# A Fourier-mixing and feed-forward kernel: one scheduling region instead of two, half of a weight conversion moved later, small copies on another engine

## The chip, the cores and the metric

The kernel runs on one core of a Trainium2 chip. The metric is device time in microseconds (us): 2882.8 us is the median of seven runs, which lie between 2877.8 and 2884.53.

A core has a matrix engine (PE in the profile; its weight loads are PEld), a vector engine (DVE), an activation engine (ACT), a general engine (POOL, GpSimd in the code) and a sync engine (SP) that here only issues transfers. Every engine takes its own instructions strictly in order, and a waiting instruction holds up all that stand behind it on that engine. Transfers are issued by SP, ACT and POOL, and all run on the core's 16 DMA engines.

## The reference

`x` has 8 batches of 3008 rows and 256 columns. The rows are transformed, multiplied by a filter, and transformed back; the result goes through a two-layer block with the activation h - tanh(h).

```python
X = np.fft.rfft(x, axis=1)
Y = X * (filt_r + 1j * filt_i)[None]
x2 = np.fft.irfft(Y, n=3008, axis=1).reshape(24064, 256)
h = x2 @ w_in                       # 256 -> 2048
out = (h - np.tanh(h)) @ w_out      # 2048 -> 256
```

`w_in`, `w_out`, and the result of the product with them, start as float64; the kernel gets the weights as 64-bit integers.

## The kernel before, in words

**The transform.** 3008 is 64 x 47. A first pass (`first0` for batch 0, `first` for the others) multiplies 64-row blocks of `x` by a constant matrix and stores the result in DRAM (`ct1`). A middle pass loads it back (`a2`), multiplies with constants (`fg`, loaded in eight slots of four matrices), applies the filter, multiplies again and stores to `ct2`. A last pass (`last`) loads `ct2` (`e2`) and multiplies once more; its result `ut` feeds the two-layer block. Batches are worked in five groups: 0, then 1 and 2, 3 and 4, 5 and 6, then 7.

**The weights.** Each weight matrix is converted from float64 bits to float32 on the chip (`converted`, L191 to L223) in jobs of 128 x 512 numbers. A job is a 512 KB load (`raw`, L197, issued by SP), DVE masks and shifts (L204, L207, L210), two ACT operations (L205, L209), a DVE step that adds the low word (L211, the last reader of `raw`), and DVE steps that assemble the result (L214, L215, L222). Two jobs make a quarter (256 of `w_in`'s or `w_out`'s 1024 paired columns or rows), and `sums` (L253) then builds four sums on POOL. Quarters 0 to 3 are `w_in`, 4 to 7 are `w_out`. `weights` (L225) is a generator: each `next` does a piece of a job, and it starts the load of a job two ahead.

**Two parts, each a region of its own** (`with tc.manual_schedule()` at L861 and at L973). Inside a region instructions stand in program order.

The *first part* does batch 0's first pass (`first0`), then a loop over j = 0 to 15 that is batch 0's middle pass. For every second j it loads the next slot of `a2` and `fg` on SP, and issues the six filter transfers two slots ahead on POOL (`filters_of`, L803, into one of three buffers). Per j there are two DVE products with the filter (`uv` L922, `zs` L923), matmuls (L896, L898, L915), an ACT copy (`e1`, L901) and its store (L902). At odd j ACT duplicates the filter rows (`double_filters`, L838) and builds a turned and negated copy of the constants (`turned`, L845, tile `gx`). One `next(ws)` per j advances the conversion of quarters 0 to 4. Near the end `first(1)` begins for the second group: two `x_sb` loads at j = 14, and after the loop EARLY = 3 of its 24 steps.

The *dense part* is a software pipeline over U, four per chunk of output columns. In step U, `up(U)` does the first product, `shrink(U-1)` the activation, `down(U-2)` the second product. Each U has five slots `t(0)` to `t(4)`. A slot can carry one step of the next group's first or middle pass (their due positions are evenly spread, `steps`), one step of the conversion of quarters 5 to 7 (`late`, at slots 0, 2 and 4), and one step of `copies` (slots 1 and 3 from U = 1 on). `copies` (`filters_d`, L951) writes zeros and then all of the filter into a DRAM tensor `filt_d`, laid out for the later middle passes: eight steps of six to ten transfers (L814), issued by SP. `down` of quarter 5 runs at U = 3, of 6 at U = 4, of 7 at U = 5; quarter 4 is used from U = 2.

In the dense part SP also issues the `x_sb` loads of `first` (two chunks ahead, three buffers), the `raw` loads (two buffers), the `e2` loads, and all output stores.

Of the kernel before, what the change touches and what calls it, by code (L numbers as in the profile page):

```python
# [41 lines left out]
EARLY = 3  # L42
# [100 lines left out]
def kernel(  # L143
# [47 lines left out]
    def converted(tiles, src, dsts, queue):  # L191
# [13 lines left out]
        ACT.activation(ft, it, AF.Identity, bias=1.0, scale=2.0 ** -20)  # L205

        V.tensor_scalar(out=pt, in0=hi, scalar1=20, scalar2=0x7FF,  # L207
                        op0=ALU.logical_shift_right, op1=ALU.bitwise_and)
        ACT.activation(pt, pt, AF.Relu, bias=exp_b)  # L209
        V.tensor_scalar(out=st, in0=hi, scalar1=-2 ** 31, scalar2=None, op0=ALU.bitwise_and)  # L210
        V.scalar_tensor_tensor(out=ft, in0=lo, scalar=2.0 ** -52, in1=ft,  # L211
                               op0=ALU.mult, op1=ALU.add)
        yield
# [11 lines left out]
    def weights(tiles, quarters, ahead):  # L225
# [36 lines left out]
        for k in range(len(jobs)):  # L262
            next(began[k])
            if k and k % 2 == 0:
                sums(quarters[k // 2 - 1])
            if k + ahead < len(jobs):
                began.append(start(k + ahead))
            yield
            next(began[k])
            yield  # L270
# [77 lines left out]
    def middle(p, z):  # L348
# [58 lines left out]
        yield  # L407

# [347 lines left out]
    with tc.tile_pool(name="tr", bufs=2) as tr:  # L756
        with tc.tile_pool(name="pro", bufs=1) as pro, \
# [45 lines left out]
            def filters_of(c, to=None):  # L803


                n = 4 if c < NK // 4 - 1 else 3

                def put(row, m, v, i, n_s, src, off, dims):
                    if to is None:
                        dst = t[IM * v + row:IM * v + row + m, v, i:i + n_s, :]  # L810
                    else:
                        dst = dram(to, ((row * 2 + v) * NK + 4 * c + i) * DM,
                                   [[2 * NK * DM, m], [DM, n_s], [1, DM]])
                    (G if to is None else nc.sync).dma_start(dst, dram(src.tensor, off, dims))  # L814

                if to is None:
                    t = filt[c % 3]


                    if c < 3:  # L820
                        for v in range(2):
                            G.memset(t[IM * v + 32:IM * v + 64, v], 0.0)
                    if n == 3:
                        G.memset(t[IM:IM + 1, 1, 3], 0.0)
                for row, m in ((0, LO), (LO, 16), (LO + 16, HI - 16)):
                    sign = 1 if row < LO else -1
                    r0 = 4 * c + 1 + NQ * row if row < LO else NQ * (row - LO + 1) - 1 - 4 * c
                    for v, src in enumerate((filt_r, filt_i)):
                        put(row, m, v, 0, n, src, r0 * DM, [[NQ * DM, m], [sign * DM, n], [1, DM]])
                if n == 3:  # L830
                    for v, src in enumerate((filt_r, filt_i)):
                        put(v, LO - v, v, 3, 1, src, v * NQ * DM,
                            [[NQ * DM, LO - v], [DM, 1], [1, DM]])
                        put(LO, HI, v, 3, 1, src, NQ // 2 * DM,
                            [[NQ * DM, HI], [DM, 1], [1, DM]])
                return None if to is not None else t
# [8 lines left out]
            def turned(g3, t):  # L845


                ACT.copy(t[0:RP], g3[IM:IM + RP])
                ACT.mul(t[IM:IM + RP], g3[0:RP], -1.0)
# [11 lines left out]
            with tc.manual_schedule():  # L861
                nc.sync.dma_start(wf1, wf1_d)
                V.memset(near_b, B)
                V.memset(exp_b, -896.0)
                xs = [load_x0(0, (0, 4, 8)), load_x0(1), load_x0(2)]
                ws = weights(tiles0, range(5), 2)

                pad = pro.tile([64, DM], F32, name="pad")
                G.memset(pad, 0.0)
                G.dma_start(dram(ct1[0], NR * 64 * DM, [[DM, 64], [1, DM]]), pad)  # L870
                fts = {0: filters_of(0)}
                gx = [pro.tile([IM + RP, 4, RP2], F32, name=f"gx{k}") for k in range(2)]
                for t in gx:
                    G.memset(t[32:64], 0.0)
                mats = {0: load_slots(0, pro)}
                next(ws)
                for c in range(3):
                    for k, _ in enumerate(first0(xs[c], c)):
                        if k == 3 or k == 1 and c > 0:
                            next(ws)  # L880
                G.dma_start(s2, s2_d)
                fts[1] = filters_of(1)
                a2 = {0: load_a2(0, 0, False)}
                mats[1] = load_slots(1, pro)
                next(ws)
                double_filters(fts[0], 0)
                turned(mats[0][1], gx[0])
                waiting = []

                def back0():  # L890
                    j, uv, zs = waiting.pop(0)
                    c = j // 2
                    pe = z0("pe", [128, 2, DM])
                    for i in range(2):
                        k = (2 * j + i) % 4
                        nc.tensor.matmul(pe[0:RP2, i], mats[c][1][:, k], uv[0:IM + RP, i],  # L896
                                         start=True, stop=False)
                        nc.tensor.matmul(pe[0:RP2, i], gx[c % 2][:, k], zs[0:IM + RP, i],  # L898
                                         start=False, stop=True)
                    e1 = tr.tile([RP2, 2, DM], F32, tag="e1", bufs=2, name="e1")  # L900
                    ACT.copy(e1, pe[0:RP2])  # L901
                    ACT.dma_start(dram(ct2[0], 2 * j * RP2 * DM,  # L902
                                       [[DM, RP2], [2 * RP * DM, 2], [1, DM]]), e1)

                for j in range(NK // 2):
                    c = j // 2
                    if j % 2 == 0 and c + 1 < NK // 4:
                        a2[c + 1] = load_a2(0, c + 1, False)
                        if c + 2 < NK // 4:
                            mats[c + 2] = load_slots(c + 2, pro)  # L910
                            fts[c + 2] = filters_of(c + 2)
                    pz = z0("pz", [128, 2, DM])
                    for i in range(2):
                        k = (2 * j + i) % 4
                        nc.tensor.matmul(pz[:, i], mats[c][0][0:R2, k],  # L915
                                         a2[c][0:R2, k * DM:k * DM + DM], start=True, stop=True)
                    if waiting:
                        back0()
                    uv = tr.tile([128, 2, DM], F32, tag="uv", bufs=2, name="uv")
                    zs = tr.tile([128, 2, DM], F32, tag="zs", bufs=2, name="zs")  # L920
                    ft = fts[c][:, :, j % 2 * 2:j % 2 * 2 + 2]
                    V.tensor_mul(uv, pz, ft[:, 0])  # L922
                    V.tensor_mul(zs, pz, ft[:, 1])  # L923
                    waiting.append((j, uv, zs))
                    next(ws, None)
                    if j % 2 and c + 1 < NK // 4:
                        double_filters(fts[c + 1], c + 1)
                        turned(mats[c + 1][1], gx[(c + 1) % 2])
                    if j == NK // 2 - 2:
                        fs = first(1, z1)  # L930
                        next(fs)
                        e2s[0] = load_e2(*groups[0], None, slice(0, 48))
                back0()
                load_e2(*groups[0], e2s[0], slice(48, 64))
                for _ in range(EARLY):
                    next(fs)
                for _ in ws:
                    pass


        with tc.tile_pool(name="dn", bufs=2) as dn, \
# [9 lines left out]
            def filters_d():  # L951
# [15 lines left out]
                for c in range(NK // 4):  # L967
                    filters_of(c, filt_d)
                    yield

            late, copies = weights(tiles1, range(5, 8), 2), filters_d()
            total = 4 * len(groups)
            with tc.manual_schedule():  # L973
                for _ in last(0, z1):
                    pass
                next(late)
                for U in range(total + 2):
                    i, u = divmod(U, 4)
                    if U < total:
                        p, c = groups[i]  # L980
                        if c == 0 and u == 0:
                            units = 4 * len(CHUNKS[p])
# [9 lines left out]
                        if u == 0 and i + 1 < len(groups) and c + 1 < len(CHUNKS[p]):  # L992
                            e2s[i + 1] = load_e2(*groups[i + 1])
# [62 lines left out]
                for w in stores:  # L1056
                    store(*w)
# [37 lines left out]
```

## Time and profile before

| | us |
|---|---|
| median of seven runs | 2882.8 |
| the profiled execution, its own time | 2883.05 |
| its span in the trace | 2881.3 |
| PE busy (share of the span) | 2752.5 (96%) |
| DVE busy | 1989.4 (69%) |
| ACT busy | 1872.1 (65%) |
| POOL busy | 1743.4 (61%) |
| first matmul of `last` (L447), where the dense part begins | 116.36 |
| mean granted clock of PE | 0.982 |

The busy share is an average over stages that have different limits. PE is busy 229.2 of the first 300 us, and 2523.3 of the 2581 us from 300 on. The windows show, for each stretch of time, the busy time of each engine with its instruction count, the granted clock of PE (1.00 is full speed), the share of time that the DMA engines worked, and what they moved. In the timeline a row is start, duration, engine, line, operation, what is written and read; "q" after an engine's name marks a transfer that it issued. In the list of waits a row names the waiting engine and line, what it waited for, and us in total, times, and the longest.

### The profile page before, as it was taken

Reading aid. Unit: us, or ns where it says so; the run is one execution under the profiler, and the core shown is the slowest. Engines: PE = TensorE matmul, PEld = TensorE weight load, DVE = VectorE, ACT = ScalarE, POOL = GpSimd, SP = SyncE. Lnnn points to the kernel's source line nnn. Section 1 sums busy time; section 2 is a strip of 40 time slices with the busy share of each in tenths; the row PEclk is TensorE's granted clock in tenths of the full one; section 3 lists DMA queues with packets and bytes.
Section 4 is the critical chain, followed back from the end, with each engine's and each line's share of the span. In section 5 each row is a group of like instructions: output and inputs, shape, how many; then the busy total and the mean of one; then the engine's idle time right before and its main releaser. Section 6 shows DMA issues by size and latency. Waiting matters only on the chain.

```text
span 2881.3 us, 36469 instructions
## 1 busy us (share of the span) xinstructions
PE 2752.5 (96%) x12474; PEld 2279.7 (79%) x12474; DVE 1989.4 (69%) x2214; ACT 1872.1 (65%) x2460; POOL 1743.4 (61%) x1382
## 2 busy tenths in 40 slices
PE   5789999999999999999999999999999999999996
PEld 3467777888878787888877887888888888888885
DVE  4675666766777777766677777776777777777765
ACT  3655666666666667666666677666666666666663
POOL 4345777444677767645576777655466666555543
PEclk7889999999999999999999999999999999999998
DMA  9644443232233322232323233122233222110100
GB/s 270 180 150 118 115 107 90 66 96 75 70 81 86 74 69 54 56 86 80 87 70 73 69 83 76 36 50 62 51 76 80 55 54 55 25 27 15 29 8 16
DMA packets 328061, 217.46 MB, mean 75 GB/s; under 512 B 229085, under 2 KB 280405, under 8 KB 327674
## 3 DMA queue, kind: packets, MB, share of 16 engines
q1 hardware_dynamic: 273176, 160.50, 23.6%
q10 hardware_dynamic: 52738, 51.33, 5.9%
q0 software_dynamic: 1952, 3.22, 0.5%
q8 instruction: 100, 1.64, 0.3%
q14 instruction: 95, 0.78, 0.1%
HBM read 138.81 MB, written 79.17 MB: 76 GB/s over the span
## 4 chain that ended last, share of the span: by engine, by line
PE 69%; ACT 9%; DVE 9%; POOL 5%; issue 4%; DMA 3%; SPq 1%; ACTq 1%; DVEq 0%; POOLq 0%
PE o L590 27%; PE x L483 18%; PE z L483 8%; PE y L483 5%; PE pe L364 3%; PE pu L447 3%; DVE h L544 3%; PE pz L383 3%; ACT y L539 2%; PE pf L304 2%; ACT y L540 1%; POOL t L465 1%; ACT u L489 1%; DVE uv L398 1%; DVE h L519 1%
## 5 line engine op out<-in xcount | busy, mean ns | idle before, releaser
L590 PE MATMUL o<-t,wd 128*128 128x256 f32 (+2 forms) x3072 | 777.2, 376 | 1.8 <-POOL t L464 1.3
L544 DVE TENSOR_TENSOR h<-h,y 128x1024 f32<-128x1024 f32 (+2 forms) x384 | 589.6, 1535 | 255.9 <-ACT y L540 255.9
L462 POOL TENSOR_TENSOR t<-h 128x512 f32<-128x512 f32 (+2 forms) x192 | 240.0, 1250 | 770.5 <-DVE h L548 584.0
L590 PEld LDWEIGHTS o<-t,wd 128*128 128x128 f32 x3072 | 580.9, 191 | 74.8 <-POOL t L464 1.9
L483 PE MATMUL x<-tu,wu 128*128 128x256 f32 (+2 forms) x2304 | 591.5, 379 | 16.5 <-ACT u L489 15.5
L590 PE MATMUL o<-h,wd 128*128 128x256 f32 (+2 forms) x2304 | 583.5, 376 | 0.2 <-DVE h L548 0.2
L548 DVE SCALAR_TENSOR_TENSOR h<-sq,h 128x1024 f32<-128x1024 f32 (+2 forms) x384 | 566.6, 1476 | 20.8 <-ACT y L539 0.5
L483 PEld LDWEIGHTS x<-tu,wu 128*128 128x128 f32 x2304 | 429.5, 191 | 157.2 <-issue 72.7
L590 PEld LDWEIGHTS o<-h,wd 128*128 128x128 f32 x2304 | 432.6, 191 | 71.9 <-issue 18.5
L545 ACT ACTIVATE sq<-y,near_b 128x1024 f32<-128x1024 f32 (+2 forms) x384 | 435.4, 1134 | 5.8 <-DVE h L548 1.1
L539 ACT ACTIVATE y<-h 128x1024 f32<-128x1024 f32 (+2 forms) x384 | 400.0, 1042 | 14.8 <-ACT e L367 6.8
L489 ACT COPY s<-x 128x512 f32<-128x512 f32 (+2 forms) x192 | 110.7, 577 | 458.3 <-PE x L483 446.9
L540 ACT ACTIVATE y<-y 128x1024 f32<-128x1024 f32 (+2 forms) x384 | 399.2, 1040 | 12.2
L465 POOL TENSOR_TENSOR t<-t,h 128x512 f32<-128x512 f32 (+2 forms) x192 | 306.8, 1598 | 0.0
L489 ACT COPY u<-x 128x512 f32<-128x512 f32 (+2 forms) x384 | 219.2, 571 | 74.9 <-PE x L483 37.8
L399 POOL TENSOR_TENSOR zs<-zs,ft 128x512 f32<-128x512 f32 x112 | 166.2, 1484 | 142.1 <-ACT zs L397 142.0
L463 POOL TENSOR_TENSOR t<-h,t 128x512 f32<-128x512 f32 (+2 forms) x192 | 241.5, 1258 | 15.1
L464 POOL TENSOR_TENSOR t<-h 128x512 f32<-128x512 f32 (+2 forms) x192 | 249.5, 1300 | 0.0
L400 POOL TENSOR_TENSOR uv<-uv,zs 128x512 f32<-128x512 f32 x112 | 211.3, 1887 | 16.0 <-DVE uv L398 7.8
L483 PE MATMUL x<-ut,wu 128*128 128x256 f32 (+2 forms) x768 | 200.5, 384 | 12.2 <-DVE h L519 10.6
L483 PE MATMUL z<-tu,wu 128*128 128x256 f32 (+2 forms) x768 | 195.9, 378 | 0.5 <-DVE h L525 0.5
L499 DVE TENSOR_TENSOR h<-y,s 128x512 f32<-128x512 f32 (+2 forms) x192 | 130.3, 679 | 94.1 <-PE y L483 85.1
(113 smaller groups left out, 3303.6 us busy)
## 6 DMA issues: line engine op xcount, KB each, us to landing
a<-ct SPq DMA_DIRECT2D x64, 384.0 KB
ct<-e ACTq DMA_DIRECT2D x128, 192.0 KB
ft<-filt SPq DMA_DIRECT2D x96, 256.0 KB
out_dram<-ot SPq DMA_DIRECT2D x1408, 16.0 KB
ct<-a ACTq DMA_DIRECT2D x80, 256.0 KB
x_sb<-in_x_dram SPq DMA_DIRECT2D x69, 256.0 KB
e<-ct SPq DMA_DIRECT2D x33, 512.0 KB
fg<-fg SPq DMA_DIRECT2D x40, 392.0 KB
```

The source lines that it names most:

```text
L462: G.tensor_sub(t[0], b[0][1], b[0][0])
L463: G.tensor_sub(t[1], b[1][1], t[0])
L464: G.tensor_sub(t[2], b[1][1], b[0][1])
L465: G.tensor_sub(t[3], t[1], b[1][0])
L483: nc.tensor.matmul(bank[:, k], wu[:, q - 1, (2 * u + k) * 128:(2 * u + k + 1) * 128], rhs[q - 1], start=(first and k == 0), stop=True, ski ...
L489: ACT.copy(t, X)
L539: ACT.activation(y[k], ht[k], AF.Arctan, scale=S)
L540: ACT.activation(y[k], y[k], AF.Square)
L544: V.tensor_mul(ht[k], ht[k], y[k])
L545: ACT.activation(sq[k], y[k], AF.Square, bias=near_b, scale=A)
L548: V.scalar_tensor_tensor(out=ht[k], in0=sq[k], scalar=K, in1=ht[k], op0=ALU.add, op1=ALU.mult)
L590: nc.tensor.matmul(product(q), wd[:, q - 1, (2 * u + k) * 128: (2 * u + k + 1) * 128], rhs[q - 1][:, k], start=(u == 0 and k == 0 and q == ...
```

## The change

1. The two regions become one that spans the whole kernel.
2. `converted` now stops once more: the three DVE masks; then the two ACT operations; then all other DVE steps, L211's among them. `weights` interleaves: a step A does the masks of job k, a step B does the ACT operations of job k, the rest of job k-1, and starts the load of job k+2.
3. The first part converts quarters 0 to 3, the dense part 4 to 7. `late` runs at every slot of U = 0 and U = 1, and at slots 0, 2 and 4 after that.
4. During `first0` the conversion takes one step instead of five; four more follow after it.
5. `turned` runs on GpSimd. The zeroing of the second and third filter buffer stands ahead of `first0`, the filter transfers of slot 1 follow the first `turned`.
6. EARLY is 2. `first(1)` starts at j = 13, `e2`'s first load is at j = 15, and the last rows of `e2` are loaded after the EARLY steps, not ahead of them.
7. `copies` writes the filter in ten transfers, over all 31 rows at once, one per step, issued by GpSimd.

```diff
-EARLY = 3
+EARLY = 2
...
         V.tensor_scalar(out=st, in0=hi, scalar1=-2 ** 31, ...)
+        yield
+        ACT.activation(ft, it, AF.Identity, bias=1.0, scale=2.0 ** -20)
+        ACT.activation(pt, pt, AF.Relu, bias=exp_b)
+        yield
         V.scalar_tensor_tensor(out=ft, in0=lo, scalar=2.0 ** -52, in1=ft, ...)
-        yield
         V.tensor_scalar_min(pt, pt, 255.0)
...
-        for k in range(len(jobs)):
-            next(began[k])
-            if k and k % 2 == 0:
-                sums(quarters[k // 2 - 1])
-            if k + ahead < len(jobs):
-                began.append(start(k + ahead))
-            yield
-            next(began[k])
-            yield
+        for k in range(len(jobs) + 1):
+            if k < len(jobs):
+                next(began[k])
+            if k > 2 and k % 2:
+                sums(quarters[k // 2 - 1])
+            yield
+            if k < len(jobs):
+                next(began[k])
+            if k > 0:
+                next(began[k - 1])
+            if k + ahead < len(jobs):
+                began.append(start(k + ahead))
+            yield
...
+    def filter_rows(a, z):
+        n, src = min(z, NK - 1) - a, (filt_r.tensor, filt_i.tensor)
+        for row, m in ((0, LO), (LO, 16), (LO + 16, HI - 16)):
+            low = row < LO
+            at = a + 1 + NQ * row if low else NQ * (row - LO + 1) - 1 - a
+            for v in range(2):
+                yield v, row, m, 0, n, dram(src[v], at * DM,
+                                            [[NQ * DM, m], [DM if low else -DM, n], [1, DM]])
...
-    with tc.tile_pool(name="tr", bufs=2) as tr:
+    with tc.tile_pool(name="tr", bufs=2) as tr, tc.manual_schedule():
...
             def turned(g3, t):
-                ACT.copy(t[0:RP], g3[IM:IM + RP])
-                ACT.mul(t[IM:IM + RP], g3[0:RP], -1.0)
+                G.tensor_copy(t[0:RP], g3[IM:IM + RP])
+                G.tensor_scalar_mul(t[IM:IM + RP], g3[0:RP], -1.0)
...
-                ws = weights(tiles0, range(5), 2)
+            ws = weights(tiles0, range(4), 2)
...
-                    if j == NK // 2 - 2:
-                        fs = first(1, z1)
-                        next(fs)
-                        e2s[0] = load_e2(*groups[0], None, slice(0, 48))
-                back0()
-                load_e2(*groups[0], e2s[0], slice(48, 64))
-                for _ in range(EARLY):
-                    next(fs)
+                if j == NK // 2 - 3:
+                    fs = first(1, z1)
+                    next(fs)
+                if j == NK // 2 - 1:
+                    e2s[0] = load_e2(*groups[0], None, slice(0, 48))
+            back0()
+            for _ in range(EARLY):
+                next(fs)
+            load_e2(*groups[0], e2s[0], slice(48, 64))
...
-                for c in range(NK // 4):
-                    filters_of(c, filt_d)
+                for v, row, m, i, n, src in filter_rows(0, NK):
+                    G.dma_start(dram(filt_d, ((row * 2 + v) * NK + i) * DM,
+                                     [[2 * NK * DM, m], [DM, n], [1, DM]]), src)
                     yield
-            late, copies = weights(tiles1, range(5, 8), 2), filters_d()
+            late, copies = weights(tiles1, range(4, 8), 2), filters_d()
...
-                        if k in (0, 2, 4):
-                            next(late, None)
-                        elif U > 0:
-                            next(copies, None)
+                    if U < 2 or k in (0, 2, 4):
+                        next(late, None)
+                    if U > 0 and k in (1, 3):
+                        next(copies, None)
```

## The prediction

> **What bounds the kernel now.** I read the windows first, because the busy shares average over stages. From 300 us on PE works 2523.3 of 2581 us, and the change touches nothing that runs there. So all that it can give or take lies in the first 300 us, of which PE works 229.2. Two windows of that stretch (PE, PEld, DVE, ACT, POOL; then clock, DMA share, GB/s):
>
> ```profile
> 0.00:50.00 50.00, 21.42 (x46) 10.70 (x47) 16.66 (x36) 16.31 (x27) 21.31 (x38) 0.76 0.97 274
> 50.00:100.00 50.00, 41.24 (x150) 26.73 (x149) 40.20 (x74) 33.06 (x49) 28.52 (x47) 0.90 0.91 236
> ```
>
> The DMA engines are taken 97% and 91% of the time, every compute engine less. The first part is bound by bytes, with DVE (40.2 of 50) next. SP's timeline shows which bytes need not be there, and how the part ends:
>
> ```profile
> 16.55 3.26 SPq L197 DMA_DIRECT2D raw<-in_moe_w_out_dram  x2
> ...
> 68.25 0.39 SPq L197 DMA_DIRECT2D raw<-in_moe_w_out_dram  x1
> ...
> 77.47 0.39 SPq L197 DMA_DIRECT2D raw<-in_moe_w_out_dram  x1
> ...
> 107.20 0.32 ACTq L902 DMA_DIRECT2D ct<-e  x1
> ...
> 110.30 1.39 SPq L283 DMA_DIRECT2D x_sb<-in_x_dram  x3
> ...
> 113.64 2.05 PE L304 MATMUL pf<-x_sb,wf_sb 128*128 128x512 f32 x2 [6.16 <-DMA x_sb<-in_x_dram]
> ```
>
> The two loads at 68.25 and 77.47 are quarter 4. The two at 16.55 can only be the first loads of `late`, because quarter 4's come far later: in program order they stand behind the whole first part, but with two regions they were put 95 us ahead of it. At the end, `x_sb` for the third EARLY step waits behind `e2`'s last rows, which wait for the store of 107.20; PE stands 6.16 us, and `last` begins only at 116.36.
>
> After that the waits of PE between 110 and 330 us, and what SP waits for between 115 and 245:
>
> ```profile
> PE pf L304 <- DMA x_sb<-in_x_dram: 12.8, 4, 6.2
> PE x L483 <- ACT u L489: 12.4, 5, 3.8
> PE pe L364 <- POOL uv L400: 4.2, 1, 4.2
> ...
> SPq L197 <- DVE ft L211: 31.4, 4, 12.5
> SPq L814 <- DMA ct<-a: 25.2, 7, 6.6
> ```
>
> The largest is a load that SP issues too late; SP's queue then holds 52 filter copies (L814), which waited 25.2 us besides their issue.
>
> **The change part by part.** The sum is made against the profiled execution, 2883.05 us, which is 0.25 us from the median; I don't correct for that.
>
> *Bytes out of the first part (one region, quarter 4 later).* Four `raw` loads of 512 KB leave it: 2.1 MB. At the mean of the two windows, 255 GB/s, that is 8.2 us; at the 399 GB/s of 20 to 30 us it is 5.3. The conversion of two jobs leaves too: by the medians of its rows 0.42 + 0.42 + 0.42 + 0.69 + 0.42 + 0.69 + 0.83 = 3.9 us of DVE a job, 7.8 in all, and 2.7 of ACT. Also, ACT no longer waits for job 0 between the copies of `first0`: it stood 8.29 us before L205 at 21.84 and the last copies came at 33.5. That and the DVE time let the loop start and end earlier, but the other bytes still have to move, so I add only 1. Bounds: 0, if the pace is set by the latency of single transfers (the `e1` store of 49.96 took 11.6 us to land); 13, because DVE at 80% lets the 64 us from 43 to 107 shrink by no more than a fifth. I take **-9**, near the byte count, as the DMA row is the fullest.
>
> *End of the first part (EARLY, order of the loads).* The two remaining EARLY steps use chunks that were loaded at j = 13. After the last `e1` store (107.20, landed at 109.48) only `e2`'s last rows come: two issues of 0.4 and a landing. The nearest landings are `x_sb`, 110.30 to 113.64, 3.3 us for four times the bytes; I take 2.5. `last` then begins at 112.3 in today's times instead of 116.36: -4. The third EARLY step moves to the dense part: two matmuls of 0.43, +0.9. Together **-3.2** (bounds -4 to -1.5, if `e2` takes as long as `x_sb` and both 0.4 issues count again).
>
> *Two more jobs in the dense part.* +7.8 us of DVE and 2.7 of ACT, all at U = 0 to U = 4 (120.99 to 213.74 today). DVE is busy 65.1 of the 80 us from 120 to 200, so 15 us are free: bounds 0 and 7.8. U = 1 gets the most: three tails (L211 to L222, 2.63 each) and two sets of masks (1.26 each), 10.4 us of DVE against some 5.8 today. I take **+4**, the middle, since idle DVE time here is mostly waiting that comes in the wrong place.
>
> *The new wait for `raw`.* L211 is the last reader of a `raw` buffer, and moves from step A of job k to step B of job k+1. With two buffers, the load of job k+2 now stands in SP's queue until then, and job k+2's masks follow one step later on DVE. Between L211 and those masks DVE has L214, L215 and L222 (1.9 us) and one to three `h` operations (0.68 each): 2.6 to 4.0 us. The load needs between 3.3 (`x_sb`, half the bytes) and 5.5 (issued 125.50, its masks ran at 130.96 without a wait). So 0 to 2.9 us a job, for six jobs: 0 to +17. Behind the masks stand `h` additions that the next `up` needs; behind the waiting load stand the `x_sb` loads. Two chunks of lead and three buffers leave an `x_sb` load about three slots. I take **+3**, half a microsecond a job, as DVE runs behind PE at U = 1 anyway.
>
> *Filter copies on GpSimd.* Of the `x_sb` stalls, 4.17 us (to 200.76) and 1.94 (to 238.27) fall where SP is among the L814 copies, and after each PE's matmul groups take 1.9 instead of 1.03 until the clock is back: some 2 us more each. That is 10 in all. SP keeps the waits of the `raw` loads up to U = 3, so I take **-7**; bounds -10 and 0. On POOL ten issues at the 0.55 us of today's L814 rows make 5.5 us, within idle stretches of 10 to 14 us a U; were they slow, the four POOL sums of `shrink` (1.3 each) would wait and PE with them.
>
> The skill's page "DMA: Bandwidth & Descriptors", section "Issuing engines are not separate DMA queues", speaks against this part: all issuers share the same DMA engines, and another issuer only saves issue time, usually small. By that rule the term would be about nothing, since no bytes go away; the SP rows above (25.2 us of waiting, 52 issues of some 0.7) say that here the issue queue is the matter.
>
> *`turned` on GpSimd.* Sixteen operations of 0.51 leave ACT (33 of 50 busy, so this gives 0). On POOL each costs between 0.35 (the memset of 32 x 1024 takes 0.94; 384 columns of it) and 1.1 (the 128 x 256 sum takes 0.73, times 1.5). At most 2.2 a slot, beside six issues (3.3) and on average 1.5 of sums: 7.0 of the 8 us a slot takes now. While POOL adds, DVE's 0.42 us masks take 0.95, so DVE may lose up to 8 us, of 27 idle in the loop. Taken: 0, bounds -1 and +4.
>
> *The zeroing and slot 1's filters earlier:* POOL is idle from 10 to 31 us. 0.
>
> Sum: -9 - 3.2 + 4 + 3 - 7 = -12.2, so 2870.8; I forecast **2870** (0.45% faster). By the terms' likelier halves this case spans 2860 to 2876.
>
> The skill's page "TensorE: Matmul & The Clock Gate", Part 1, says that an idle window of some 3.4 us halves the clock; the 1.94 us stall, after which groups also took about twice as long, is shorter than that. By the page that stall would cost 2 and not 4 us.
>
> **Rivals.**
> (a) *The front is not bound by bytes*: the freed DMA time goes to latency, and the loop keeps its pace. For it: the 11.6 us landing, and DMA at 45% already at 95 us. Against: 0.97. Then -3.2 + 4 + 3 - 7 = -3: 2880, no change that can be told.
> (b) *The conversion becomes a chain* (the other side): each of six jobs waits for its load behind the job two before it, DVE stands in front of `h`, and `x_sb` is late behind the same load. For it: SP already waits 31.4 us for L211. Price: +17 from the loads; then the -7 is lost too, as SP stays blocked, and one cold start (2) is added: -9 - 3.2 + 4 + 17 + 2 = +11: 2894. It decides from a load of about 5 us on, where the wait exceeds 2 us a job.
> (c) *The front gains more*: loop down to DVE's pace (-13), hidden conversion (0), no new wait, all SP stalls gone: -13 - 3.2 - 10 = -26, so 2857.
> (d) *It doesn't do what it says*: one region changes nothing, and `late`'s loads still come early. Then half of the byte term (4.1) returns: 2875, inside the main case.
>
> **How the numbers follow.** Main case with (d) 0.60, (c) 0.13, (a) 0.15, (b) 0.12. A difference of 0.2% (5.8 us) is about what a measurement tells from none; the bounds are 2877 and 2888.6. Faster: main and (c), 0.73; same: (a), 0.15; slower: (b), 0.12. The range goes from 2853 ((c) with the outer bounds -4 and -1, and one cold start less, -30 in all) to 2887, which holds (a) and leaves out (b).
>
> **What would show it.** Right: no `w_out` load before the dense part; first `a<-ct` load before 34 us (38.28 now); last `e1` store near 98; `last` within 5.5 us of it; no L814 on SP, and PE's `x_sb` waits after that below 4 us; DVE waits for `raw` under 5 us in all. Wrong: the last `e1` store later than 104; a long DVE wait for `raw`; PE waiting for `h` or `x_sb` at U = 0 to 3 more than the 25 us it stands between 116 and 300 now.

## The result and the profile after

The changed kernel takes 2890.99 us, the median of 13 runs (2885.67 to 2898.0), against 2881.09 of the kernel before on the same chips. The ratio is 1.0033, interval 1.0026 to 1.004: it is slower by some 9.5 us, where 2870 was forecast. Its profiled execution took 2889.44 us, with a span of 2887.7.

The loss lies where the prediction looked, in the first 300 us: PE works 225.55 of them (229.21 before), and from the eighth `up` (U = 7) to the last but three the two traces run 9.5 to 10.1 us apart. In the last three U, which the change does not touch, 3.2 us of that go again (granted clock over the last five U 0.94 before, 0.98 after), so that the two spans differ by only 6.4; the size of the change is taken from the ratio. The stages, with the first part's end and the start of each U's `y` product read from PE's timeline:

| us from the start | before | after |
|---|---|---|
| first `pz` matmul of the first part | 43.19 | 38.97 |
| first `uv` on DVE | 45.32 | 44.95 |
| last `e1` store | 107.20 | 104.54 |
| first matmul of `last` | 116.36 | 110.84 |
| U = 0 | 122.69 | 117.17 |
| U = 7 | 246.50 | 256.27 |
| from U = 0 to U = 7 | 123.8 | 139.1 |

So the first part gives 5.5 us, and the first seven U take 15.3 more. 5.5 less and 15.3 more make 9.8.

**The first part.** The same two windows as before (PE, PEld, DVE, ACT, POOL; clock, DMA share, GB/s):

```profile
0.00:50.00 50.00, 21.10 (x44) 10.62 (x45) 10.77 (x26) 14.22 (x23) 21.14 (x37) 0.74 0.86 241
50.00:100.00 50.00, 40.99 (x160) 28.27 (x159) 40.07 (x71) 27.85 (x38) 42.24 (x64) 0.92 0.92 236
```

The bytes did leave the first 50 us (DMA share 0.86, it was 0.97), but the second window is as full as before. The timeline of SP, then that of DVE, show why the loop does not start five microseconds earlier with them:

```profile
34.28 0.33 SPq L340 DMA_DIRECT2D a<-ct  x1
...
35.12 1.20 SPq L197 DMA_DIRECT2D raw<-in_moe_w_in_dram  x2
```

```profile
34.26 0.76 DVE L223 SCALAR_TENSOR_TENSOR wu<-conv 128x256 f32<-128x256 f32 x2
43.94 0.43 DVE L204 TENSOR_SCALAR conv<-raw 128x512 int32<-128x512 int32 x1 [8.91 <-issue]
...
44.95 0.68 DVE L926 TENSOR_TENSOR uv<-pz,filt 128x512 f32<-128x512 f32 x1
```

`pz` is 4.2 us earlier and `uv` only 0.4: DVE stands 8.9 us in front of job 2's masks, whose load SP issued only at 35.12, behind the first `a<-ct` (the row itself names no releaser; raw_first, below, tries it). In the kernel before seven `raw` loads were issued ahead of that `a<-ct`, and five behind it; now it is two and six. One region took the two loads of `late` out, and the later quarter took two out of the loop; but the conversion that starts later pushed three `w_in` loads into the loop.

**The dense part.** The waits of PE from 110 to 330 us, and what SP waits for from 115 to 245:

```profile
PE pf L309 <- DMA x_sb<-in_x_dram: 12.0, 3, 4.8
PE pu L469 <- DMA e<-ct: 5.2, 1, 5.2
...
PE z L505 <- DVE h L547: 3.6, 1, 3.6
...
PE o L612 <- POOL wd L258: 2.7, 1, 2.7
```

```profile
SPq L288 <- PE pf L309: 46.3, 10, 12.2
SPq L197 <- DVE pt L215: 37.3, 4, 13.6
SPq L197 <- DVE ft L213: 17.3, 2, 12.7
```

Before, the 12.8 us of `x_sb` held 6.2 that belong to the end of the first part; 6.6 lay in the dense part. Now all 12.0 do. The filter copies (L814, 25.2 us of SP) are gone, and the waits of the `raw` loads (L197) grew from 31.4 us for four loads to 54.6 for six. Four of the waits name L215, the operation behind the last reader L213, but SP issues each of the six loads 0.03 to 0.04 us after an end of L213. The largest row shows no loss: there `x_sb` loads that SP reaches early wait for a buffer that PE still reads (three_raw, below, has 57.8 us of it, and PE never waits for `x_sb`). How the two hang together is read from the second of the three stalls, in the timelines of DVE, SP and PE:

```profile
163.84 0.68 DVE L213 SCALAR_TENSOR_TENSOR ft<-raw,ft 128x512 f32<-128x512 uint32 x1
```

```profile
164.55 0.40 SPq L197 DMA_DIRECT2D raw<-in_moe_w_out_dram  x1
165.06 2.94 SPq L288 DMA_DIRECT2D x_sb<-in_x_dram  x2
```

```profile
170.41 2.08 PE L309 MATMUL pf<-x_sb,wf_sb 128*128 128x512 f32 x2 [2.75 <-DMA x_sb<-in_x_dram]
```

DVE ends the last reader of a `raw` buffer; at once SP issues the load that had waited for that buffer; at once after it the `x_sb` load that stood behind; 5.3 us later PE can go on. The other two stalls have the same form: `raw` at 131.92, `x_sb` at 132.80, PE idle 4.76 to 138.25; `raw` at 180.81, `x_sb` at 181.28, PE idle 4.48 to 185.49. From 160 to 180 and from 180 to 200 us the granted clock is 0.83 (before: 1.00 and 0.83).

### The profile page after: what moved, and what is told of

Its sections match the earlier page's. It is cut to its first block, busy times and chain, and to the rows that moved or that the text cites. A ratio compares the mean times of both kernels' runs of the same rounds, so it can differ in the third digit from the quotient of the medians.

```text
span 2887.7 us, 36447 instructions
## 1 busy us (share of the span) xinstructions
PE 2753.3 (95%) x12474; PEld 2281.1 (79%) x12474; DVE 1988.6 (69%) x2214; ACT 1864.8 (65%) x2444; POOL 1766.9 (61%) x1408
## 4 chain that ended last, share of the span: by engine, by line
PE 70%; DVE 9%; ACT 8%; POOL 5%; issue 4%; DMA 3%; ACTq 1%; SPq 0%; DVEq 0%; POOLq 0%
PE o L612 27%; PE x L505 18%; PE z L505 8%; PE y L505 5%; PE pe L369 3%; PE pu L469 3%; DVE h L566 3%; PE pz L388 3%; ACT y L561 2%; PE pf L309 2%; POOL t L487 1%; ACT y L562 1%; DVE h L570 1%; ACT u L511 1%; DVE uv L403 1%
## 5 line engine op out<-in xcount | busy, mean ns | idle before, releaser
L561 ACT ACTIVATE y<-h 128x1024 f32<-128x1024 f32 (+2 forms) x384 | 400.0, 1042 | 15.3 <-ACT e L372 7.3
L562 ACT ACTIVATE y<-y 128x1024 f32<-128x1024 f32 (+2 forms) x384 | 399.2, 1040 | 12.2
L505 PE MATMUL y<-ut,wu 128*128 128x256 f32 (+2 forms) x768 | 195.5, 377 | 0.0
```

Of the source, the lines that this page charges most:

```text
L505: nc.tensor.matmul(bank[:, k], wu[:, q - 1, (2 * u + k) * 128:(2 * u + k + 1) * 128], rhs[q - 1], start=(first and k == 0), stop=True, ski ...
L561: ACT.activation(y[k], ht[k], AF.Arctan, scale=S)
L562: ACT.activation(y[k], y[k], AF.Square)
```

## The experiments

Two theories. **L:** a `raw` buffer now lives from its load until the step B of the next job, two buffers are too few for that, and what waits is not the conversion but SP, with `x_sb` behind it. **W:** the dense part has two more jobs and does not hide them. A third question was where the 9 us of the first part went. All ratios below are against the kernel before on the same chip (2879.07 to 2880.64 us).

**short_life**: in the dense part the conversion with the old lifetime of `raw` (and the old loop over its jobs), all else as in the changed kernel.

```diff
 V.tensor_scalar(out=st, in0=hi, ...)
-yield
+if not short:
+    yield
 ACT.activation(ft, it, AF.Identity, bias=1.0, scale=2.0 ** -20)
 ACT.activation(pt, pt, AF.Relu, bias=exp_b)
-yield
+if not short:
+    yield
 V.scalar_tensor_tensor(out=ft, in0=lo, scalar=2.0 ** -52, in1=ft, ...)
+if short:
+    yield
...
-late = weights(tiles1, range(4, 8), 2)
+late = weights(tiles1, range(4, 8), 2, True)
```

> The changed kernel, but the dense part converts as before: masks, ACT operations and L211 of a job in one step, the rest in the next, so that a raw buffer and an ft buffer are held for one step less. Theory L (the longer life of the buffers makes SP and ACT wait, and x_sb comes late behind raw): the stretch from the first matmul of last to U = 7, 145.4 us in the changed kernel and 130.1 before, falls to 132 or less, PE's waits for x_sb in it from 12.0 to under 5, and the ratio to the kernel before from 1.0033 to between 0.997 and 1.000. Theory W (the 7.8 us of DVE, 2.7 of ACT and 3 of POOL that came into this stretch cost it): the stretch stays above 142 and the ratio above 1.002.

Measured: 2880.27 us, ratio 0.9999 (0.9989 to 1.001). PE has no wait for `x_sb` left in the dense part. The loss goes with the longer life, though the two additional jobs are still there: L. The life of `ft` is shorter here too, so that `raw` alone is not shown by this run. The profiled execution (2875.13) is 5 us below this median, so I read no size of a stage from it.

**zero_apart**: the `zero` tile of `copies` shares its buffers with the conversion's `ft` in the changed kernel; here it has one of its own.

```diff
-zero = tr.tile([128, 4 * DM], F32, tag="a2", bufs=2, name="zero")
+zero = dn.tile([128, 4 * DM], F32, tag="ot", bufs=1, name="zero")
```

> The changed kernel with the tile of zeros in a buffer of its own and not in one of the two that ft uses. If the two ft buffers are the main part of theory L (ACT stood 9.7 us before L210 at 156.55), that wait goes, U = 2 falls from 26.6 us by 6 or more, ratio about 1.001. If raw in SP's queue is the main part, the three waits of PE for x_sb (4.8, 2.8, 4.5) stay and the ratio falls by no more than 0.001. Theory W: no change.

Measured: 2889.89 us, ratio 1.0036 (1.0023 to 1.0048); `x_sb` waits 12.8. These buffers are not the cause.

**three_raw**: zero_apart with a third `raw` buffer in the dense part, so that it differs from zero_apart in this alone.

```diff
+if k == "raw" and job % 3 == 2:
+    return dn.tile([128, n], dtype, tag="o", bufs=1, name=k)
```

> The changed kernel with the zeros apart as in zero_apart, and a third raw buffer for the dense part, so that the load of job k+2 waits for job k-1 and not for job k. All the conversion's work stays. Theory L: PE's waits for x_sb fall under 4 us, the stretch to U = 7 falls from 145.4 to 132 or less, ratio 0.997 to 1.000. Theory W: the stretch stays above 142, ratio above 1.002.

Measured: 2875.28 us, ratio 0.9982 (0.9973 to 0.9992): 14.6 us below zero_apart. The largest waits of PE in the same stretch, without any for `x_sb`:

```profile
PE x L505 <- ACT u L511: 6.1, 4, 4.9
...
PE z L505 <- DVE h L547: 5.7, 2, 3.7
...
PE o L612 <- POOL wd L258: 2.7, 1, 2.7
```

From U = 0 to U = 7 it takes 122.0 us instead of 135.8 (139.1 in the changed kernel), with a clock of 0.96 and 0.91 from 160 to 180 and from 180 to 200. A buffer of 512 KB is worth more than the whole change cost.

**turned_act**: the changed kernel with `turned` on ACT, as before.

```diff
-G.tensor_copy(t[0:RP], g3[IM:IM + RP])
-G.tensor_scalar_mul(t[IM:IM + RP], g3[0:RP], -1.0)
+ACT.copy(t[0:RP], g3[IM:IM + RP])
+ACT.mul(t[IM:IM + RP], g3[0:RP], -1.0)
```

> The changed kernel with the turned matrices on ACT again. If POOL paces the loop of the first part (it is busy 42 of the 50 us from 50 to 100, against 28.5 before), the loop, 65.6 us from its first matmul to the last e1 store, shortens by 3 us or more and the ratio falls by 0.001. If the loop is paced by transfers, it stays within 1.5 us.

Measured: 2890.43 us, ratio 1.0037 (1.0024 to 1.0051). The loop of the first part, from the first `pz` to the last `e1` store, takes 68.0 us, 65.6 with `turned` on POOL: nothing shows that POOL, though it is busy 42 of 50 us there, paces the loop.

**one_region**: the kernel before, its two regions made one.

```diff
-with tc.tile_pool(name="tr", bufs=2) as tr:
+with tc.tile_pool(name="tr", bufs=2) as tr, tc.manual_schedule():
```

> The kernel before with one thing changed: one region in program order instead of two, so that the first two w_out loads of the dense part come only there. The step 'bytes out of the first part', as the prediction counted it, takes these two loads (1 MB) as 4.1 us less for the DMA engines, so the first a<-ct load should come near 34 us and the time fall to about 2876 (before on a chip is about 2880). The rival, that the first part is paced by the order and the latency of its transfers and not by their sum, expects the last e1 store within 1.5 us of 107.2, and a time of 2879 to 2883, since what is saved there is waited for again when the loads come late in the dense part.

Measured: 2879.26 us, ratio 1.0003 (0.9993 to 1.0012). The first `pz` starts at 43.10 (43.19 before), the last store at 106.47: the 1 MB that goes (both loads now come at 110.96, behind the first part) was not what it waited for.

**copies_pool**: the kernel before, with the filter copies as ten transfers of GpSimd.

```diff
-for c in range(NK // 4):
-    filters_of(c, filt_d)
+for v, row, m, i, n, src in filter_rows(0, NK):
+    G.dma_start(dram(filt_d, ...), src)
```

> The kernel before with one thing changed: the filter copies of the dense part are ten transfers of GpSimd's queue instead of 52 of SP's. The prediction's step expects that SP's wait of 25.2 us in the copies goes, with it the x_sb stalls of 4.17 and 1.94 us and their cold starts: -7, so about 2873. By the rule of the page 'DMA: Bandwidth & Descriptors' that it cited, another issuer saves next to nothing: 2880. A third reading, that large transfers delay the small ones, expects x_sb landings longer than 6 us and a time above 2882.

Measured: 2875.85 us, ratio 0.9989 (0.998 to 0.9999): -3.2 us. In the waits of PE (110 to 330) what is left of `x_sb` is the one at the end of the first part:

```profile
PE pf L304 <- DMA x_sb<-in_x_dram: 5.5, 1, 5.5
```

So the mechanism was as forecast, and less than half of the 7 us that it was priced at. From U = 0 to U = 7 it takes 113.7 us, one_region 119.6, and the kernel before 123.8 in the profiled execution, which at 2883.05 us lies 2 us above the median of its runs here: the stalls that the 7 was read from may not all be usual ones. The rule of the Trainium skill's page "DMA: Bandwidth & Descriptors" ("Issuing engines are not separate DMA queues") would have given about nothing. The interval excludes that only narrowly; the vanished stalls speak against it too.

**raw_gpsimd**: the changed kernel with the dense part's `raw` loads issued by GpSimd.

```diff
-late = weights(tiles1, range(4, 8), 2)
+late = weights(tiles1, range(4, 8), 2, G)
```

> The changed kernel, with the raw loads of the dense part issued by GpSimd instead of SP; the two buffers and the order of the conversion stay. If the price is that x_sb stands in SP's queue behind a load that waits for its buffer, PE's waits for x_sb between 110 and 260 us (12.0 in the changed kernel) fall below 4; the wait for the buffer then stands in GpSimd's queue instead, ahead of the sums of shrink, so PE's waits for POOL rise from 2.7, and the time is 2878 to 2890, by which of the two is shorter. If the price is the late conversion itself (the masks late in front of h on DVE), the x_sb waits do not matter and the time stays at 2889 to 2891.

Measured: 2882.94 us, ratio 1.0016 (1.0006 to 1.0025). The largest wait of PE, 110 to 330 (the waits for `x_sb`, 12.0 in the changed kernel, are down to 0.5):

```profile
PE x L505 <- ACT u L511: 10.6, 5, 4.9
```

The buffers are still two, yet `x_sb` is in time: it was SP's queue that made it late. By the ratios this returns 4.9 of the 14.6 us (from U = 0 to U = 7: 129.4). The rest is not split further: GpSimd now waits 39.2 us for the buffers, and PE's waits for ACT rise from 3.0 to 10.6; whether those come of that or of the late conversion was not tried apart. So the queue of SP is shown to make `x_sb` late, and not to be the whole price.

**early_raw**: three_raw, with three loads ahead in the first part.

```diff
-ws = weights(tiles0, range(4), 2)
+ws = weights(tiles0, range(4), 3)
```

> The kernel of three_raw (2875.3) with one number changed: the first part starts three raw loads ahead instead of two. In the changed kernel loads 2 and 3 stand in SP's queue behind the first a<-ct load, which waits until 34.28, so that the DMA engines are taken only 76% and 65% of 30 to 50 us, and the masks of job 2, which wait for load 2 (until 43.94), stand on DVE ahead of the first uv (44.95), six microseconds after the first pz matmul. If this order is where the expected gain of the first part went, the first uv comes by 42, the last e1 store 2 to 4 us earlier than 104.5, and the time is 2871 to 2873.5. If the first part is bound by the sum of its bytes, the early load only takes the place of others: first uv and last store unchanged within 1 us, 2875.

Measured: 2881.15 us, ratio 1.0012 (1.0002 to 1.0022): a miss, 6 us above three_raw. The first `uv` does come at 41.63, but now load 4 waits for its buffer in SP's queue, ahead of the second `a<-ct` (SP's timeline):

```profile
35.41 0.33 SPq L340 DMA_DIRECT2D a<-ct  x1
...
36.25 7.83 SPq L197 DMA_DIRECT2D raw<-in_moe_w_in_dram  x2
44.13 0.60 SPq L340 DMA_DIRECT2D a<-ct  x1
```

That second `a` came at 36.46 in three_raw. The DMA share of 50 to 70 falls to 0.55 and 0.59, and the last `e1` store comes at 113.75. (The profiled execution, 2885.95 us, is 4.8 above the median; the order of the loads does not depend on that.) It is L again, in the other part.

**raw_first**: three_raw, with only the third load ahead of the first `a<-ct`; its buffer is free.

```diff
+next(ws)
 G.dma_start(s2, s2_d)
...
-for _ in range(4):
+for _ in range(3):
     next(ws)
```

> The kernel of three_raw with the third raw load of the first part issued before the first a<-ct load instead of after it (it goes to the third buffer, which is free, so SP does not stand). Only loads 0 to 2 come early; load 3, which early_raw also drew forward and which stood 7.8 us in SP's queue for its buffer, keeps its place. If the first uv is late because the masks of job 2 wait for load 2, uv comes by 42.5 (44.4 in three_raw), the last e1 store 1 to 3 us earlier, and the time is 2872 to 2874.5 against a before of 2879 to 2880. If the loop is bound by its bytes or by the chain from filter load to uv, uv is earlier and the last store is not: 2875.

Measured: 2871.14 us, ratio 0.9965 (0.9951 to 0.9978). First `uv` 41.19, last `e1` store 103.15, first matmul of `last` 109.70. The loop from the first `pz` to the last store takes 64.1 us (67.5 in three_raw). (The step that is drawn forward also holds job 0's two ACT operations.) The time is 4.9 us below three_raw by the ratios, whose intervals just overlap; back_and_first, below, has the same step once more.

**masks_later**: three_raw, with one step of the conversion less ahead of the loop, so that job 2's masks stand behind the first `uv`.

```diff
-for _ in range(4):
+for _ in range(3):
     next(ws)
 double_filters(fts[0], 0)
```

> The kernel of three_raw with three instead of four steps of the conversion ahead of the loop of the first part, so that the masks of job 2 stand on DVE behind the first uv and zs, not ahead of them; every later step comes one slot later. No byte and no load changes its place ahead of the loop. If the wait of DVE for load 2 is what costs, the first uv comes by 41.5 and the last e1 store 1 to 3 us earlier: 2872 to 2874.5. If the loop is bound by bytes, the three microseconds are waited for again at the next filter or a load: 2875, within 1 us.

Measured: 2873.98 us, ratio 0.9975 (0.9966 to 0.9984). First `uv` 40.46, last `e1` store 106.81. The loop takes 68.5 us: an earlier `uv` alone is not seen at its end. The time is 1.3 us below three_raw's, with intervals that overlap, so no gain is shown.

**both_first**: the two edits together.

```diff
+next(ws)
 G.dma_start(s2, s2_d)
...
-for _ in range(4):
+for _ in range(2):
     next(ws)
```

> The two edits of raw_first and masks_later together: the third raw load ahead of the first a<-ct load, and the masks of job 2 behind the first uv. If the two only reach the same end (DVE free for the first uv), the time is that of the better of the two, within 1 us. If the early bytes help by themselves, because the DMA engines are taken only three quarters of 30 to 50 us, it is 1 to 2 us below the better of the two.

Measured: 2875.54 us, ratio 0.9987 (0.9978 to 0.9996): neither of the two outcomes expected. It lies above raw_first (the intervals just touch) and can't be told from masks_later. The last `e1` store comes at 111.61 (in an execution 2.9 us above the median), and DVE waits 18.3 us for doubled filters (L836, on ACT) in the loop, 12.2 in masks_later and 9.4 in raw_first. In masks_later and both_first the steps of the conversion fall on other parities of j, so ACT's part of it comes ahead of `double_filters`; that this is why was not tried by itself.

**quarter_back**: three_raw, with quarter 4 in the first part again.

```diff
-ws = weights(tiles0, range(4), 2)
+ws = weights(tiles0, range(5), 2)
...
-late = weights(tiles1, range(4, 8), 2)
+late = weights(tiles1, range(5, 8), 2)
```

> The kernel of three_raw with quarter 4 converted in the first part again, as in the kernel before (ten jobs there, six in the dense part). The prediction's terms say that this returns two loads (1 MB) to the first part, +4.1, and takes two jobs from the dense part, -4: no change, 2875. If the first part is not bound by bytes and the dense part hides nothing, the two jobs are worth 4 us there: 2871. If the first part has to drain the two jobs behind its loop, in front of last, the last e1 store and the first pu are 4 to 8 us later: 2878 to 2882.

Measured: 2868.07 us, ratio 0.9953 (0.9939 to 0.9966). `last` begins at 114.32 and the stretch from U = 0 to U = 7 takes 110.5 (122.0 in three_raw). Of the waits of PE that stood behind the two jobs, those for `h` and for quarter 7's sums (5.7 and 2.7 in three_raw), this is left:

```profile
PE z L505 <- DVE h L547: 2.0, 1, 2.0
```

So there is something in W after all: a second cause, which the third buffer had left standing.

**quarter_two**: the changed kernel with quarter 4 back, and its two `raw` buffers.

```diff
-ws = weights(tiles0, range(4), 2)
+ws = weights(tiles0, range(5), 2)
...
-late = weights(tiles1, range(4, 8), 2)
+late = weights(tiles1, range(5, 8), 2)
```

> The changed kernel with quarter 4 back in the first part, but with its two raw buffers (quarter_back has three and took 2868.1). It tells whether the price of the two buffers belongs to each job or to the two jobs too many. If each job pays its share of what the third buffer saved with eight jobs (2889.9 - 2875.3 = 14.6), six jobs pay 11: 2879, with PE's waits for x_sb near 9 us between 116 and 330. If only the crowd of eight jobs at U = 0 to 4 makes the load late, the time is 2868 to 2871 and x_sb waits are below 2.

Measured: 2873.24 us, ratio 0.9973 (0.9964 to 0.9982), between the two expectations. The largest wait of PE, 110 to 330, and the one for `x_sb`:

```profile
PE pf L309 <- ACT a L310: 5.8, 2, 5.3
...
PE pf L309 <- DMA x_sb<-in_x_dram: 3.3, 2, 2.9
```

Two buffers instead of three cost 5.2 us here (5.8 by the ratios, whose intervals just overlap; the `zero` tile also differs, which cost nothing measurable above), 0.9 a job; with eight jobs it was 14.6, or 1.8 a job. So the two causes are not independent: with more jobs the missing buffer costs more for each. By what path was not tried apart.

**back_and_first**: quarter_back with, in addition, the edit of raw_first.

```diff
+next(ws)
 G.dma_start(s2, s2_d)
...
-for _ in range(4):
+for _ in range(3):
     next(ws)
```

> The kernel of quarter_back with the edit of raw_first (third raw load of the first part ahead of the first a<-ct load). If what each gave holds side by side (raw_first 4.1 below three_raw, of which 3.2 are seen at the first pu), the first pu comes by 111.5 (114.32 in quarter_back) and the time is 2864 to 2866. If the first part, with quarter 4's bytes in it again, is bound by the bytes, the early start is lost by the end of the loop: 2868.

Measured: 2863.11 us, ratio 0.9938 (0.9924 to 0.9952). `last` begins at 110.61. By the ratios the early load gave 4.9 us on three_raw and gives 4.3 here: the intervals overlap both times, but sign and size are the same twice, with a megabyte more in the loop the second time. It is the fastest kernel of this study, 17.5 us below the kernel before: the change, with one more `raw` buffer, without the later quarter, and with one load ahead of the wait for `ct`.

## Why the prediction was wrong, step by step

To size the steps, one spread has to be known: of five executions whose first part is the changed kernel's (after, short_life, zero_apart, three_raw, raw_gpsimd) the last `e1` store comes between 103.1 and 108.1 and the first matmul of `last` between 109.5 and 113.7. Three with (nearly) the first part of before end it at 106.5 to 107.2, and begin `last` at 115.8 to 116.4.

*Bytes out of the first part, -9.* Mis-sized. The mean of the last store goes from 106.9 to 105.2: -1.8. The loop does start earlier (first `pz` 43.1 to 38.3 in the mean, -4.8) but then takes longer: 65.4 to 70.4 us from the first `pz` to the last store in the five, 63.4 to 64.3 in the three, +3.0 in the mean. With one load put back ahead of the first `a<-ct` it takes 64.1 and 64.3 (raw_first, back_and_first), so it fits that the `w_in` loads which the changed order pushed into the loop took the gain back. One region alone gave nothing (+0.2 us). What quarter 4's megabyte is worth stays inside the spread: with it the last store is 3.0 us later in one comparison (quarter_back and quarter_two, 107.6 and 108.8) and 0.6 in another (back_and_first, 103.7). What failed is "as the DMA row is the fullest": 0.97 told that the queues held work then, and not that the loop was waiting for its last byte. In windows of 10 us the changed kernel's DMA share is 0.76 from 30 to 40 and 0.65 from 40 to 50, where the loop stands for load 2. The prediction counted the loads that leave and did not count those that move behind the first `a<-ct`. Rival (a) describes this term best.

*End of the first part, -3.2.* Right, within its bounds. From the last store to `last` it was 9.2 to 9.3 and is 5.6 to 6.8: -3.1 in the mean, where the forecast had -4. With the 0.9 for the third EARLY step, which no run measures alone, that is -2.2.

*Two more jobs in the dense part, +4 (0 to 7.8).* Too low, and by the traces out of its bounds: 11.5 us from U = 0 to U = 7 in three_raw and quarter_back. The other five traces with three buffers in the dense part say 9 to 12 (119.5 to 122.4 with the two jobs, 110.8 without); by the ratios it is 8.4 for the whole kernel, the quarter's cost in the first part included. The upper bound was DVE's own time of the two jobs. That is no bound: PE stands 7.2 us more in the stretch, 6.4 of them for `h` and for quarter 7's sums by the rows above, and its busy time grows by 4.3 us for the same 397 matmuls (granted clock 0.92 instead of 0.95).

*The new wait for `raw`, +3 (0 to +17).* **This is the step that failed most**: 14.6 us (zero_apart to three_raw). It was named, its bounds held, and rival (b) had the price. Wrong was the value, half a microsecond a job, because I took it as a wait of DVE and put the `x_sb` loads behind it at nothing. In the dense part DVE itself waits 1.0 us for `raw`; SP stands 54.6 us behind the two buffers, and PE 12.0 for the `x_sb` loads behind that. With the `raw` loads off SP's queue 4.9 of the 14.6 came back, while GpSimd's queue stood 39.2 us instead; by what path the rest is paid stays open. "Two chunks of lead and three buffers leave an `x_sb` load about three slots" did not hold against waits of up to 13.6 us, which the 12.5 in before's own list (L211) had foretold.

*Filter copies on GpSimd, -7.* Right in mechanism: L814 leaves SP, and with it the stalls of PE. Alone it is worth 3.2 (0.3 to 5.8), within its bounds. (After the stall of 1.94 us a group of four took 1.43 us and one of eight 3.22, not quite twice their usual 1.03 and 1.89: some 1.7 us more, where the prediction had 2.) Whether it is lost in the changed kernel, as (b) said, no run shows: none puts the copies back on SP there.

*`turned`: 0.* Right (1.0037 without it, 1.0033 with it). An operation on POOL took 0.49 to 0.61 (the copy) and 1.16 to 1.24 (the multiplication).

So (b), at 0.12, was the case: its "+17 from the loads" is 14.6. Its "-7 is lost" is not shown, and of its two ways "`x_sb` is late" is the one that the stalls show: 12.0 us, against 3.6 and 1.7 in the two rows for `h`. That its sum, 2894, came near is partly luck: its -9 was 7.2 too much, and it took 4 for the two jobs, 7.5 too little. The terms as measured are -1.8 (bytes) - 2.2 (end) + 11.5 (jobs) + 14.6 (buffers), 22.1; the change gave 9.5. Of the other 12.6, the copies are 3.2 by their own run and 6 to 10 by the traces from U = 0 to U = 7 (113.7 against 119.6 and 123.8). Quarter_back, with 110.5, is another 3 below copies_pool, which may be the finer steps of the conversion. Executions of one kernel differ by several us, and the sum can't be closed further; what of these 12.6 us is whose stays open.

## What to carry to other kernels

A load that waits for a buffer was here a wait for every transfer behind it on the same issuing engine. When a change delays the last reader of a buffer, ask first what stands behind the next load of that buffer, and count buffers by their lifetime in steps: here one more was worth 14.6 us. And a full DMA row (0.97 here) does not show that a stage is bound by its bytes; look at which loads are issued ahead of the first wait, and how many, before and after.

## What the runs showed of the hardware

DVE operations grow long beside POOL's additions. In the changed kernel the tail of one job runs with POOL idle at first, the next beside four sums of POOL (150.05 to 156.17); DVE's timeline:

```profile
142.07 0.69 DVE L216 SCALAR_TENSOR_TENSOR pt<-pt,st 128x512 int32<-128x512 int32 x1
142.80 0.83 DVE L223 SCALAR_TENSOR_TENSOR wd<-ft,pt 128x256 f32<-128x256 f32 x3
...
152.01 1.64 DVE L216 SCALAR_TENSOR_TENSOR pt<-pt,st 128x512 int32<-128x512 int32 x1
153.68 2.84 DVE L223 SCALAR_TENSOR_TENSOR wd<-ft,pt 128x256 f32<-128x256 f32 x3
```

The same two lines take 1.52 and 4.48 us. The prediction had 0.95 for a mask of 0.42 under this load, and 3.9 us for a job's whole DVE work; in this place these two lines alone take longer. It may be one reason why two more jobs cost more than their own time; that was not tried.

PE's clock falls after a short idle stretch. Around the stall of 2.75 us at 170.41, in the windows of the changed kernel (PE, PEld, DVE, ACT, POOL; then clock, DMA share, GB/s):

```profile
164.00:168.00 4.00, 3.66 (x17) 2.87 (x16) 2.63 (x7) 3.97 (x7) 0.00 (x0) 1.00 0.82 259
...
170.50:175.00 4.50, 4.50 (x11) 3.04 (x12) 0.88 (x2) 0.58 (x1) 0.00 (x0) 0.63 0.18 60
```

The two `pf` matmuls take 2.08 us there, the next two, at 174.78, 1.02. The Trainium skill's page "TensorE: Matmul & The Clock Gate" (Part 1) that the prediction cited has some 3.4 us for the idle window; 2.75 was enough here. So a stall costs PE more than its own length. How much shows in the stretch from U = 0 to U = 7, first of the changed kernel, then of three_raw:

```profile
117.17:256.27 139.10, 112.94 (x398) 82.90 (x396) 95.73 (x133) 73.83 (x100) 55.83 (x55) 0.86 0.44 139
```

```profile
119.27:241.25 121.98, 104.53 (x397) 78.10 (x396) 95.42 (x133) 73.87 (x100) 56.10 (x55) 0.92 0.49 154
```

Of the 17.1 us between the two, 8.7 are idle time of PE and 8.4 are the same matmuls, run longer at a lower clock.
